# The end of the last token group: order of the sums, columns in two banks, stores of 64 rows

## The chip, the cores and the metric

The kernel runs on one core of a Trainium2 chip. A core has five engines with a queue each: TensorE (PE, matrix products; its weight loads are listed as PEld), VectorE (DVE), ScalarE (ACT), GpSimd (POOL) and SyncE (SP, which only issues transfers here). Transfers are carried by 16 DMA engines that all queues share. The metric is the device time of one execution in microseconds (us), as the median of several runs.

## What is computed

The reference is one block of a network over 2048 tokens of 512 channels: a normalisation with a modulation, a long convolution per channel (computed through a spectrum), a gated residual, and a second normalisation followed by a mixer. What matters for this change is the end of it, the channel MLP of the mixer, in float32:

```python
h2 = _gelu(_layernorm(x1, axis=-1) @ w3) @ w4      # w3: 512 x 1376, w4: 1376 x 512
return x1 + h2
...
x = x + gb * _B_ref(h, B_w1, B_w2, B_w3, B_w4)     # gb: one factor per channel
```

## The kernel before, in words

The tokens lie in one SBUF tile, `X2` (in the profile `KX`), as 128 partitions x 16 blocks x 512 channels. Partition `bp * 32 + q` of block `b` holds token `q * 64 + bp * 16 + b`. In DRAM the output has one row of 512 floats (2 KB) per token, so that the 32 partitions of one `bp` in one block are 32 rows that lie 64 rows (128 KB) apart, and the next `bp` begins 16 rows further on.

The last stage, from about 430 us on, is a loop over eight groups of 256 tokens (`chan(g, hl)`, lines 966 to 1067); a group is two blocks, its two token halves `i = 0, 1` of 128 tokens. The order of the work is written out by hand, and each engine takes its instructions in program order. A group does:

- `chan_first` (922 to 934), called as `first(f2)` for f2 = 0 to 5: the product with w3 for 256 of the 1376 hidden channels (96 in the last, f2 = 5) and all 256 tokens. Each product is made of three (`three`, 822 to 828), since every operand is held as a rounded part (`h`) and a rest (`l`): h x h, l x h and h x l, with 256 columns each. Then ScalarE evaluates GELU twice (into `gh`, rounded, and `gf`) and VectorE subtracts (`gl`, line 933).
- `chan_second` (951 to 955), called as `second(f2)`: the product with w4. For each token half `i` one PSUM bank, `acc[i]` (`pa` in the profile), collects the sums of all 11 hidden tiles; a product has 128 tokens as its stationary side and 512 output channels as its columns. `second_high` (936 to 942) adds the two products with `gh`, `second_low` (944 to 949) the one with `gl`. In `chan_second` the order is high of half 0, high of half 1, low of half 0, low of half 1.
- `chan_out` (957 to 964) for each half: VectorE multiplies the sums by the factors `mods[5]` into a scratch tile (line 960) and adds them to the block of `X2` (line 961); then four stores of 32 rows go to the output (line 963), one for each `bp`. In groups 0 to 6 all are issued on SP, in group 7 alternately on SP and ACT.

Between these, a group prepares the next one: `chan_split`, `chan_mod`, `chan_w2`, `chan_stats`, `chan_norm`, `chan_add`, and in groups 1 to 3 a piece of the token mixing, whose results go to a scratch tensor in DRAM (`GD`, line 837) and come back as windows (`chan_load`, line 860). Those transfers are on SP, in the same queue as the stores. `chan_sum` (874) sums the product with w2 in a bank named `ph`.

In group 7 the end is written out (lines 1059 to 1064): after `first(5)` come the high products of part 4 for both halves, then for half 0 low of part 4, high and low of part 5, then the same for half 1; part 4 has two hidden tiles, part 5 one. Only then both halves' `chan_out` follow.

How a store's address pattern is written: `dram(t, offset, [[step, count], ...])` gives steps and counts from the outermost to the innermost, so `[[64 * 512, 32], [1, 512]]` are 32 rows of 512 floats. Loads and stores elsewhere have 128, 96, 64, 32 or 16 as their outermost count, and the four loads into `DS` (line 331), one row each, have 1.

Of the kernel before, what the change touches and what calls it, by code (L numbers as in the profile page):

```python
# [7 lines left out]
F32 = mybir.dt.float32  # L8
# [99 lines left out]
def dram(t, off, ap):  # L108
    return bass.AP(tensor=t.tensor, offset=t.offset + off, ap=ap)


def body(ctx, tc, A):
    nc = tc.nc
    V, S, P, T, Y = nc.vector, nc.scalar, nc.gpsimd, nc.tensor, nc.sync
# [63 lines left out]
    X2 = KX.rearrange("p (b d) -> p b d", b=16)  # L178
# [9 lines left out]
    ph = a1.enter_context(pool("ph"))  # L188
# [14 lines left out]
    mods = [modu[:, k] for k in range(3)] + [modg[:, k] for k in range(3)]  # L203
# [73 lines left out]
    f2 = lambda t: t.rearrange("p a b -> p (a b)")  # L277
# [190 lines left out]
    def products(k):  # L468
        t, u = divmod(k, 4)
        tr = trig.pop(k)  # L470
        mg = PE[t][0][u]
        e0 = wk.tile([128, 2, 2, 512], F32, name="e0")
        e1 = wk.tile([128, 2, 16, 32], F32, name="e1")
        for a in range(2):
            V.scalar_tensor_tensor(e0[:, 1, a], tr[:, 1, 0], 1.0 - 2.0 * a, mg[:, a], op0=OP.mult, op1=OP.mult)  # L475
        if k == 0:
            weigh(0)
        if u % 2 == 0:
            m1 = m1s[0] = wk1.tile([128, 2, 512], F32, name="m1")
            pt = PE[t][1][:, u:u + 2].rearrange("p a d c -> p (a d) c")  # L480
            V.tensor_mul(m1.rearrange("p a (d x y) -> p (a d) x y", x=4, y=8),
                         pt[:, :, None, :8].to_broadcast([128, 32, 4, 8]),
                         pt[:, :, 8:12, None].to_broadcast([128, 32, 4, 8]))
        V.tensor_mul(e0[:, 0], tr[:, 0, 0:1].to_broadcast([128, 2, 512]), mg)  # L484
        V.tensor_mul(e1.rearrange("p r d q -> p r (d q)"), tr[:, :, 1], m1s[0][:, u % 2:u % 2 + 1].to_broadcast([128, 2, 512]))  # L485
        return e0, e1
# [29 lines left out]
    for k in range(8):  # L516
        w, i = ("w3", k) if k < 4 else ("w4", k - 4)
# [21 lines left out]
    with tc.manual_schedule():  # L539
# [13 lines left out]
        for k in range(33):  # L553
# [8 lines left out]
            if k < 32:  # L562
# [3 lines left out]
                e = products(k)  # L566
# [236 lines left out]
    def mix_mod1(g):  # L803
        mh[g] = (cm.tile([128, 2, 512], F32, name="h2"), cm.tile([128, 2, 2], F32, name="mv"),
                 cm.tile([128, 2], F32, name="rs"), cm.tile([128, 2], F32, name="nm"))
        for i in range(2):
            mod1(mh[g][0][:, i], 2 * g + i)

    def mix_mod2(g, i):
        h, mv, r, nm = mh[g]  # L810
        mod2(h[:, i], 2 * g + i)
        stats(mv[:, i], h[:, i])
        rstd(r[:, i:i + 1], mv[:, i, 1:2])
        P.tensor_tensor(nm[:, i:i + 1], mv[:, i, 0:1], m_one[:, :1], op=OP.mult)
        P.tensor_tensor(nm[:, i:i + 1], nm[:, i:i + 1], r[:, i:i + 1], op=OP.mult)

    def mix_norm(g):
        h, mv, r, nm = mh[g]
        for i in range(2):
            act(h[:, i], h[:, i], AF.Identity, scale=r[:, i:i + 1], bias=nm[:, i:i + 1])  # L820
# [101 lines left out]
    def chan_first(hl, f2):  # L922
        p = psw.tile([128, 2, 256], F32, name="pm")
        ne, m = (2, 128) if f2 < 5 else (1, 96)
        for e in range(ne):
            c = slice((f2 * 2 + e) * 128, (f2 * 2 + e) * 128 + m)
            three(p[:m, e], W3h, W3l, hl, c)
        gf = c2p.tile([128, 2, 256], F32, name="gf")
        gh = c2p.tile([128, 2, 256], F32R, name="gh")
        gl = c2p.tile([128, 2, 256], F32R, name="gl")  # L930
        act(gh[:m, :ne], p[:m, :ne], AF.Gelu_apprx_tanh)
        act(gf[:m, :ne], p[:m, :ne], AF.Gelu_apprx_tanh)
        V.tensor_sub(gl[:m, :ne], gf[:m, :ne], gh[:m, :ne].bitcast(F32))  # L933
        return gh, gl, ne, m

    def second_high(acc, part, f2, i):
        gh, gl, ne, m = part
        s = slice(i * 128, i * 128 + 128)
        for e in range(ne):
            f = f2 * 2 + e  # L940
            T.matmul(acc[i], gh[:m, e, s], W4h[:m, f], start=(f == 0), stop=False)  # L941
            T.matmul(acc[i], gh[:m, e, s], W4l[:m, f], start=False, stop=False)  # L942

    def second_low(acc, part, f2, i):
        gh, gl, ne, m = part
        s = slice(i * 128, i * 128 + 128)
        for e in range(ne):
            f = f2 * 2 + e
            T.matmul(acc[i], gl[:m, e, s], W4h[:m, f], start=False, stop=(f == 10))  # L949

    def chan_second(acc, part, f2):
        for i in range(2):
            second_high(acc, part, f2, i)
        for i in range(2):
            second_low(acc, part, f2, i)

    def chan_out(g, acc, i, qs):
        b = 2 * g + i
        o = c2p.tile([128, 512], F32, name="gf")
        V.tensor_mul(o, acc[i], mods[5])  # L960
        V.tensor_add(X2[:, b], X2[:, b], o)
        for bp in range(4):
            qs[bp % len(qs)].dma_start(dram(A["out"], (bp * 16 + b) * 512, [[64 * 512, 32], [1, 512]]),
                                       X2[bp * 32:(bp + 1) * 32, b])

    def chan(g, hl):
        t = g + 3 if 0 < g < 4 else None
        nx = g + 1 if g < 7 else None
        acc = [psm.tile([128, 512], F32, name=f"pa{i}", bufs=1) for i in range(2)]
        part, st = {}, {}  # L970

        def first(f2):
            part[f2] = chan_first(hl, f2)

        def second(f2):
            chan_second(acc, part.pop(f2), f2)

        def mod(i):
            if t is not None:
                if i == 0:  # L980
                    mix_mod1(t)
                    mix_mod2(t, 0)
                else:
                    mix_mod2(t, 1)
                    mix_norm(t)

        def turn():
            if t is not None:
                st["hl"] = parts_of(transposed(mh.pop(t)[0]))

        def half(hf):
            if t is not None:
                mix_half(t, st["hl"], hf)
                if t < 6:
                    first_stat(2 * t + 2 + hf)

        def nxt(f, *a):
            if nx is not None:
                return f(nx, *a)

        if g == 0:
            first(0)
            split_w(4)
            first(1)
            split_w(2)
            second(0)
            chan_split(1)
            first(2)
            split_w(2)
            chan_mod(1, 0)  # L1010
            second(1)
            chan_mod(1, 1)
            first(3)
            split_w(4)
            second(2)
            chan_w2(1)
            chan_stats(1)
            first(4)
            n = chan_norm(1)
            split_w(3)  # L1020
            second(3)
            chan_add(1)
            first(5)
            r = parts_of(transposed(n))
            second(4)
            chan_load(2)
            second(5)
        else:
            first(0)
            mod(0)  # L1030
            first(1)
            mod(1)
            second(0)
            nxt(chan_split)
            first(2)
            nxt(chan_mod, 0)
            second(1)
            turn()
            nxt(chan_mod, 1)
            first(3)  # L1040
            half(0)
            second(2)
            nxt(chan_w2)
            nxt(chan_stats)
            first(4)
            n = nxt(chan_norm)
            nxt(chan_add)
            half(1)
            second(3)
            first(5)  # L1050
            r = parts_of(transposed(n)) if nx is not None else None
            if g < 7:
                second(4)
            if g < 6:
                chan_load(g + 2)
            if g < 7:
                second(5)
            else:
                second_high(acc, part[4], 4, 0)
                second_high(acc, part[4], 4, 1)  # L1060
                for i in range(2):
                    second_low(acc, part[4], 4, i)
                    second_high(acc, part[5], 5, i)
                    second_low(acc, part[5], 5, i)
        for i in range(2):
            chan_out(g, acc, i, (Y,) if g < 7 else (Y, S))
        return r

    splits = []
# [8 lines left out]
    def split_w(n):  # L1078
        for _ in range(n):
            splits.pop(0)()  # L1080

    steps = [(jh, kc) for jh in range(2) for kc in range(8)]
    with tc.manual_schedule():
# [115 lines left out]
        W4h, W4l, ldw4 = weights(pw34, WD["w4"], 1376, 512, "w4", 11)  # L1199
        c2p = ctx.enter_context(tp("c2p", 2))  # L1200
        psm = ctx.enter_context(tp("psm", 2, space=PSUM))
# [69 lines left out]
```

## Time and profile before

| | |
|---|---|
| median of 3 runs | 711.11 us (710.77 to 711.17) |
| the profiled execution's own time | 710.0 us |
| its span in the profile | 708.2 us |
| mean granted TensorE clock | 0.996 |
| DMA traffic | 85.51 MB, mean 121 GB/s |
| the 64 stores of the output | 64 KB each, 60 on SP and 4 on ACT |

The span is the time from the first to the last instruction of the profiled execution; the execution's own time has 1.8 us around it. In rows of the timeline the columns are start, duration, engine, line, operation, output and inputs, shapes, count, and in brackets the engine's idle time before it with what ended it; equal neighbours are merged, so that a row with x3 covers three. "SPq" and "ACTq" are issues of transfers by these engines' queues. In rows of windows the columns are the window, its length, busy time and number of instructions of PE, PEld, DVE, ACT and POOL, the granted clock, the busy share of the 16 DMA engines and their GB/s. In strips (DMA, GB/s) a window is cut into 40 equal slices; a digit is the busy share in tenths. Packets are what the DMA engines move one by one: a row of an output store is a packet, and beside these there are small ones of under 512 bytes that carry no output.

### The profile page before, as it was taken

Reading aid. Unit: us, or ns where it says so; the run is one execution under the profiler, and the core shown is the slowest. Engines: PE = TensorE matmul, PEld = TensorE weight load, DVE = VectorE, ACT = ScalarE, POOL = GpSimd, SP = SyncE. Lnnn points to the kernel's source line nnn. Section 1 sums busy time; section 2 is a strip of 40 time slices with the busy share of each in tenths; the row PEclk is TensorE's granted clock in tenths of the full one; section 3 lists DMA queues with packets and bytes.
Section 4 is the critical chain, followed back from the end, with each engine's and each line's share of the span. In section 5 each row is a group of like instructions: output and inputs, shape, how many; then the busy total and the mean of one; then the engine's idle time right before and its main releaser. Section 6 shows DMA issues by size and latency. Waiting matters only on the chain.

```text
span 708.2 us, 16836 instructions
## 1 busy us (share of the span) xinstructions
PE 670.5 (95%) x7083; PEld 518.3 (73%) x7083; DVE 500.1 (71%) x827; ACT 336.0 (47%) x553; POOL 91.5 (13%) x203
## 2 busy tenths in 40 slices
PE   1899999999999999997999899999999999999997
PEld 0456655666568655654788789899898988989896
DVE  7799999999986765776988868467454536354522
ACT  3878898889956454542444633314132221212120
POOL 4011112021000000000563101001020000000000
PEclk9999999999999999999999999999999999999999
DMA  8903274745349997965559211011110201111011
GB/s 285 285 2 83 65 219 117 199 103 174 84 105 348 252 274 259 300 208 184 189 187 321 65 31 31 16 45 31 39 52 16 60 16 36 25 31 31 0 31 31
DMA packets 56627, 85.51 MB, mean 121 GB/s; under 512 B 5508, under 2 KB 43400, under 8 KB 54888
## 3 DMA queue, kind: packets, MB, share of 16 engines
q1 hardware_dynamic: 52536, 66.87, 33.4%
q0 software_dynamic: 3136, 16.52, 6.7%
q8 instruction: 56, 0.92, 0.6%
q10 hardware_dynamic: 880, 1.05, 0.5%
q14 instruction: 19, 0.16, 0.1%
HBM read 58.20 MB, written 31.85 MB: 127 GB/s over the span
## 4 chain that ended last, share of the span: by engine, by line
PE 46%; DMA 4%; DVE 2%; ACT 1%; SPq 1%; issue 1%; ACTq 0%; DVEq 0%
PE pm L825 7%; PE pm L826 7%; PE pm L828 7%; PE pa L949 6%; PE pa L941 6%; PE pa L942 6%; PE ph L880 2%; PE ph L882 2%; PE ph L879 2%; DMA GD<-go 2%; PE pT L790 2%; DMA ld<-ZT 1%; DMA w4l<-Dw 1%; PE pT L1139 1%; SPq L738 1%
## 5 line engine op out<-in xcount | busy, mean ns | idle before, releaser
L120 ACT ACTIVATE gh<-pm 128x512 fp32r<-128x512 f32 (+1 forms) x48 | 26.9, 561 | 200.6 <-PE pm L828 200.6
L825 PE MATMUL pm<-nh,w3h 128*128 128x256 f32 (+1 forms) x352 | 85.8, 279 | 0.9 <-ACT nh L120 0.9
L826 PE MATMUL pm<-nh,w3l 128*128 128x256 f32 (+1 forms) x352 | 85.7, 279 | 0.1
L933 DVE TENSOR_TENSOR gl<-gf,gh 128x512 fp32r<-128x512 f32 (+1 forms) x48 | 30.8, 642 | 68.4 <-ACT gf L120 68.4
L941 PE MATMUL pa<-w4h,gh 128*128 128x512 f32 (+1 forms) x176 | 69.6, 396 | 0.0
L942 PE MATMUL pa<-w4l,gh 128*128 128x512 f32 (+1 forms) x176 | 68.9, 392 | 0.0
L825 PEld LDWEIGHTS pm<-nh,w3h 128*128 128x128 f32 (+1 forms) x352 | 65.3, 185 | 2.6 <-ACT nh L120 1.1
L826 PEld LDWEIGHTS pm<-nh,w3l 128*128 128x128 f32 (+1 forms) x352 | 65.3, 185 | 2.2 <-DVE w3l L744 0.5
L828 PE MATMUL pm<-nl,w3h 128*128 128x256 f32 (+1 forms) x352 | 54.8, 277 | 0.0
L949 PE MATMUL pa<-w4h,gl 128*128 128x512 f32 (+1 forms) x176 | 48.1, 390 | 0.8 <-DVE gl L933 0.8
L457 PE MATMUL xx<-MG,ON 64*128 64x512 f32 x160 | 48.1, 397 | 0.0
L458 PE MATMUL xx<-MG,ON 64*128 64x512 f32 x160 | 48.0, 396 | 0.0
L753 POOL TENSOR_TENSOR rs<-mv,eps_t 128x1 f32<-128x1 f32 (+1 forms) x39 | 11.9, 306 | 277.8 <-DVE mv L759 265.8
L828 PEld LDWEIGHTS pm<-nl,w3h 128*128 128x128 f32 (+1 forms) x352 | 46.7, 185 | 0.2 <-DVE nl L798 0.2
L885 DVE TENSOR_TENSOR h<-h,ph 128x512 f32<-128x512 f32 x16 | 11.0, 687 | 45.1 <-PE ph L882 45.1
L475 DVE SCALAR_TENSOR_TENSOR e<-tr,p 128x512 f32<-128x512 f32 x64 | 41.0, 682 | 1.5 <-ACT tr L120 1.4
L120 ACT ACTIVATE z<-pz 128x512 f32<-128x512 f32 x32 | 17.4, 595 | 51.9 <-issue 25.1
L678 DVE TENSOR_TENSOR ma<-pk,us 128x512 f32<-128x512 f32 x32 | 21.9, 685 | 27.3 <-issue 16.1
L507 PEld LDWEIGHTS kp<-e,e 128*32 128x32 f32 x2048 | 30.1, 110 | 12.7 <-issue 8.2
L949 PEld LDWEIGHTS pa<-w4h,gl 128*128 128x128 f32 (+1 forms) x176 | 33.0, 188 | 8.3 <-DVE gl L933 1.2
L484 DVE TENSOR_TENSOR e<-tr,p 128x1024 f32<-128x1024 f32 x32 | 38.9, 1216 | 0.0
L485 DVE TENSOR_TENSOR e<-tr,m 128x1024 f32<-128x1024 f32 x32 | 38.9, 1216 | 0.0
(230 smaller groups left out, 1758.3 us busy)
## 6 DMA issues: line engine op xcount, KB each, us to landing
VU<-vs SPq DMA_DIRECT2D x64, 128.0 KB, 3.4
ld<-VU SPq DMA_DIRECT2D x16, 512.0 KB, 14.5
ZT<-z POOLq DMA_DIRECT2D x15, 512.0 KB, 6.3
ld<-ZT SPq DMA_DIRECT2D x12, 512.0 KB, 6.2
Dw<-in_w POOLq DMA_DIRECT2D x8, 688.0 KB, 4.7
xu<-in_u SPq DMA_DIRECT2D x16, 256.0 KB, 8.1
KX<-in_u SPq DMA_DIRECT2D x16, 256.0 KB, 12.6
GD<-go SPq DMA_DIRECT2D x16, 256.0 KB, 2.2
```

Of the source, the lines that this page charges most:

```text
L120: return S.activation(out, in_, f, bias=bias, scale=scale)
L457: T.matmul(x[:, :512], la, ma, start=(i == 0), stop=(i == len(ops) - 1))
L458: T.matmul(x[:, 512:], lb, mb, start=(i == 0), stop=(i == len(ops) - 1))
L475: V.scalar_tensor_tensor(e0[:, 1, a], tr[:, 1, 0], 1.0 - 2.0 * a, mg[:, a], op0=OP.mult, op1=OP.mult)
L484: V.tensor_mul(e0[:, 0], tr[:, 0, 0:1].to_broadcast([128, 2, 512]), mg)
L485: V.tensor_mul(e1.rearrange("p r d q -> p r (d q)"), tr[:, :, 1], m1s[0][:, u % 2:u % 2 + 1].to_broadcast([128, 2, 512]))
L825: T.matmul(p, wh[:, k, c], hi[k], start=(k == 0), stop=False)
L826: T.matmul(p, wl[:, k, c], hi[k], start=False, stop=False)
L828: T.matmul(p, wh[:, k, c], lo[k], start=False, stop=(k == 3))
L941: T.matmul(acc[i], gh[:m, e, s], W4h[:m, f], start=(f == 0), stop=False)
L942: T.matmul(acc[i], gh[:m, e, s], W4l[:m, f], start=False, stop=False)
L949: T.matmul(acc[i], gl[:m, e, s], W4h[:m, f], start=False, stop=(f == 10))
```

## The change

In group 7 the sums of the second half are kept in two banks: columns 0 to 255 in the old `acc[1]`, columns 256 to 511 in a tile of the `ph` buffers (`acc[3]`). Products of the second half therefore have 256 columns, and there are twice as many. The parts of the last group are (half 0, 512 columns), (half 1, columns 0 to 255), (half 1, columns 256 to 511).

After `first(5)` each part in turn gets all that is left of its sums (high and low of part 4, high and low of part 5), and its `chan_out` follows at once: multiply, add and stores of that part alone.

In all groups `chan_out` stores 64 partitions at a time instead of 32: the address pattern in DRAM gets a dimension in front, `[2, 32, columns]`, for two neighbouring `bp`. In groups 0 to 6 a half has two stores on SP instead of four; in group 7 each part has one on SP and one on ACT.

```diff
-    def second_high(acc, part, f2, i):
+    def second_high(acc, part, f2, i, c=slice(0, 512)):
         gh, gl, ne, m = part
-        s = slice(i * 128, i * 128 + 128)
+        s = slice(i % 2 * 128, i % 2 * 128 + 128)
         for e in range(ne):
             f = f2 * 2 + e
-            T.matmul(acc[i], gh[:m, e, s], W4h[:m, f], start=(f == 0), stop=False)
-            T.matmul(acc[i], gh[:m, e, s], W4l[:m, f], start=False, stop=False)
+            T.matmul(acc[i][:, c], gh[:m, e, s], W4h[:m, f, c], start=(f == 0), stop=False)
+            T.matmul(acc[i][:, c], gh[:m, e, s], W4l[:m, f, c], start=False, stop=False)
...
+    halves = [(0, slice(0, 512)), (1, slice(0, 256)), (3, slice(256, 512))]
 
     def chan_second(acc, part, f2):
-        for i in range(2):
-            second_high(acc, part, f2, i)
-        for i in range(2):
-            second_low(acc, part, f2, i)
-
-    def chan_out(g, acc, i, qs):
-        b = 2 * g + i
+        todo = halves if len(acc) > 2 else [(0, slice(0, 512)), (1, slice(0, 512))]
+        for i, c in todo:
+            second_high(acc, part, f2, i, c)
+        for i, c in todo:
+            second_low(acc, part, f2, i, c)
+
+    def chan_out(g, acc, i, c=slice(0, 512)):
+        b = 2 * g + i % 2
         o = c2p.tile([128, 512], F32, name="gf")
-        V.tensor_mul(o, acc[i], mods[5])
-        V.tensor_add(X2[:, b], X2[:, b], o)
-        for bp in range(4):
-            qs[bp % len(qs)].dma_start(dram(A["out"], (bp * 16 + b) * 512, [[64 * 512, 32], [1, 512]]),
-                                       X2[bp * 32:(bp + 1) * 32, b])
+        V.tensor_mul(o[:, c], acc[i][:, c], mods[5][:, c])
+        V.tensor_add(X2[:, b, c], X2[:, b, c], o[:, c])
+        for h in range(2):
+            (Y, Y if g < 7 else S)[h].dma_start(
+                dram(A["out"], (h * 32 + b) * 512 + c.start, [[16 * 512, 2], [64 * 512, 32], [1, c.stop - c.start]]),
+                X2[h * 64:h * 64 + 64, b, c])
 
     def chan(g, hl):
...
         acc = [psm.tile([128, 512], F32, name=f"pa{i}", bufs=1) for i in range(2)]
+        if g == 7:
+            acc += [None, psm.tile([128, 512], F32, name="ph")]
...
-                second_high(acc, part[4], 4, 0)
-                second_high(acc, part[4], 4, 1)
-                for i in range(2):
-                    second_low(acc, part[4], 4, i)
-                    second_high(acc, part[5], 5, i)
-                    second_low(acc, part[5], 5, i)
-        for i in range(2):
-            chan_out(g, acc, i, (Y,) if g < 7 else (Y, S))
+                for i, c in halves:
+                    second_high(acc, part[4], 4, i, c)
+                    second_low(acc, part[4], 4, i, c)
+                    second_high(acc, part[5], 5, i, c)
+                    second_low(acc, part[5], 5, i, c)
+                    chan_out(g, acc, i, c)
+        for i in range(2 if g < 7 else 0):
+            chan_out(g, acc, i)
         return r
```

`second_low` is changed like `second_high`.

More of the change, by code (lines that the diff above doesn't have):

```diff
@@ L934, in chan_first @@
         return gh, gl, ne, m
-    def second_high(acc, part, f2, i):
+    def second_high(acc, part, f2, i, c=slice(0, 512)):
         gh, gl, ne, m = part
-        s = slice(i * 128, i * 128 + 128)
+        s = slice(i % 2 * 128, i % 2 * 128 + 128)
         for e in range(ne):
             f = f2 * 2 + e
-            T.matmul(acc[i], gh[:m, e, s], W4h[:m, f], start=(f == 0), stop=False)
-            T.matmul(acc[i], gh[:m, e, s], W4l[:m, f], start=False, stop=False)
-    def second_low(acc, part, f2, i):
+            T.matmul(acc[i][:, c], gh[:m, e, s], W4h[:m, f, c], start=(f == 0), stop=False)
+            T.matmul(acc[i][:, c], gh[:m, e, s], W4l[:m, f, c], start=False, stop=False)
@@ L945, in second_low @@
+    def second_low(acc, part, f2, i, c=slice(0, 512)):
         gh, gl, ne, m = part
-        s = slice(i * 128, i * 128 + 128)
+        s = slice(i % 2 * 128, i % 2 * 128 + 128)
         for e in range(ne):
             f = f2 * 2 + e
-            T.matmul(acc[i], gl[:m, e, s], W4h[:m, f], start=False, stop=(f == 10))
+            T.matmul(acc[i][:, c], gl[:m, e, s], W4h[:m, f, c], start=False, stop=(f == 10))
+    halves = [(0, slice(0, 512)), (1, slice(0, 256)), (3, slice(256, 512))]
     def chan_second(acc, part, f2):
-        for i in range(2):
-            second_high(acc, part, f2, i)
```

## The prediction

> **What bounds the kernel now.** I read the profile's page first, then the busy time by windows of the last stage, then the timeline of the tail, then the DMA views.
>
> ```profile
> span 708.2 us, 16836 instructions
> PE 670.5 (95%) x7083; PEld 518.3 (73%) x7083; DVE 500.1 (71%) x827; ACT 336.0 (47%) x553; POOL 91.5 (13%) x203
> ```
>
> TensorE is busy for 95% of the span. In windows of 15 us from 415 to 700 (first and last of 19 rows; the first number after the window's length is PE's) it never stops:
>
> ```profile
> 415.00:430.00 15.00, 15.00 (x89) 13.13 (x88) 9.20 (x19) 4.29 (x10) 0.90 (x2) 1.00 0.13 36
> ...
> 685.00:700.00 15.00, 15.00 (x97) 13.57 (x96) 2.38 (x4) 2.83 (x6) 0.00 (x0) 1.00 0.01 1
> ```
>
> So in groups 0 to 6 the stores, adds and loads lie beside TensorE, and only what changes TensorE's own time counts there. After 700 it is a chain: the end of the sums, VectorE, the stores, their landing. The timeline of the tail:
>
> ```profile
> 699.58 0.42 DVE L933 TENSOR_TENSOR gl<-gf,gh 96x256 fp32r<-96x256 f32 x1 [3.03 <-ACT gf L120]
> ...
> 700.53 0.61 PE L949 MATMUL pa<-w4h,gl 128*128 128x512 f32 x2
> ...
> 701.88 0.69 DVE L960 TENSOR_TENSOR gf<-pa,modg 128x512 f32<-128x512 f32 x1 [1.87 <-PE pa L949]
> ...
> 702.60 0.69 DVE L961 TENSOR_TENSOR KX<-KX,gf 128x512 f32<-128x512 f32 x1
> 702.60 0.39 PE L949 MATMUL pa<-w4h,gl 96*128 96x512 f32 x1
> 703.21 0.68 DVE L960 TENSOR_TENSOR gf<-pa,modg 128x512 f32<-128x512 f32 x1
> 703.32 2.16 SPq L963 DMA_DIRECT2D out<-KX  x4
> 703.33 2.17 ACTq L963 DMA_DIRECT2D out<-KX  x4
> 703.93 0.69 DVE L961 TENSOR_TENSOR KX<-KX,gf 128x512 f32<-128x512 f32 x1
> ```
>
> TensorE ends at 702.99 (702.60 + 0.39), VectorE only at 704.62: from 701.88 on VectorE is the chain. The last issue is ACT's at 705.1; its row below says 2.0 us to landing, so 707.1, and the span ends 1.1 later. Then the DMA strips from 703 to 708.2 (40 slices of 0.13 us) and the row with the highest rate:
>
> ```profile
> L963 ACTq DMA_DIRECT2D out<-KX x2: 374/403/432, 704.6 to 705.1; - x2
> ...
> DMA to landing us min/median/max: 2.0/2.0/2.0
> DMA  0000000047999699913798949995100000000000
> ...
> DMA packets 384, 0.52 MB, mean 101 GB/s; under 512 B 128, under 2 KB 128, under 8 KB 384
> 706.00:706.50 0.50, 0.00 (x0) 0.00 (x0) 0.00 (x0) 0.00 (x0) 0.00 (x0) 0.50 0.96 238
> ```
>
> The data starts in slice 8, near 704.07, 0.75 after the issue at 703.32, and is all but through with slice 27, at 706.6: 1.6 us lie between the end of the data and the end of the span. Eight stores left 384 packets: 256 of 2 KB (8 x 32 rows) and 128 small ones, 16 for each store.
>
> **The change part by part.** *Sums in two banks.* In group 7 the 33 products of the second half (11 tiles x 3) become 66 of 256 columns. Prices:
>
> ```profile
> 691.79 0.28 PE L825 MATMUL pm<-nh,w3h 128*128 128x256 f32 x1
> ...
> 694.54 0.39 PE L941 MATMUL pa<-w4h,gh 128*128 128x512 f32 x1
> ...
> 697.28 0.28 PE L825 MATMUL pm<-nh,w3h 128*96 128x256 f32 x1
> ...
> 698.70 0.39 PE L941 MATMUL pa<-w4h,gh 128*128 128x512 f32 x1
> ```
>
> From 691.79 to 694.54 ran 24 products of 256 columns (0.1146 us each), from there to 697.28 twelve of 512 (0.2283). So 66 x 0.1146 - 33 x 0.2283 = +0.03 us. The 96-wide stage up to 698.70, 12 in 1.42 us, is the upper end (+0.27); a gain is excluded, since the same columns stream. I take 0.03, the same form.
>
> *First half first.* Its last product now stands behind 9 products instead of 13, four fewer: 0.91 us earlier. It needs gl of the last part, ready at 700.00 and used at 700.53; that cover of 0.53 us is enough. The first multiply starts at 701.88 - 0.91 + 0.03 = 701.00, the first add at 701.72, its end is 702.41, the store's issue 702.44 instead of 703.32.
>
> *Each part by itself.* VectorE's queue is then mul, add of 512 and twice mul, add of 256; a 256-wide one takes:
>
> ```profile
> L265 DVE TENSOR_TENSOR p<-p,WN 128x256 f32<-128x256 f32 x8 | 3.3, 418 | 0.4 <-ACT WN L120 0.4
> ```
>
> With the steps of the tail (0.72, 0.61, 0.72 at 512, each 0.27 less at 256): 702.33, 702.78 (end 703.20), 703.12, 703.57 (end 703.99). TensorE is through with the first quarter by 702.0 and with the second by 703.02, so VectorE stays the chain by 0.1 us. Issues at 702.44, 703.22 and 704.01 on SP and on ACT, the last 1.1 before today's. Behind each waiting store stand only the later stores and the final waits. Second add and first quarter's store touch other columns of one block; bounds 0 and a wait, taken as 0 (third rival).
>
> *Stores of 64 rows.* Here lies the sum. The new address pattern in DRAM is 2 x 32 rows: its outermost count is 2. Today's is 32. What says how many of the 16 engines carry a transfer? The list of all DMA issues:
>
> ```profile
> DMA packets 56627, 85.51 MB, mean 121 GB/s; under 512 B 5508, under 2 KB 43400, under 8 KB 54888
> ...
> VU<-vs SPq DMA_DIRECT2D x64, 128.0 KB, 3.4
> ...
> DS<-in_dk SPq DMA_DIRECT2D x4, 0.5 KB
> ld<-in_ld SPq DMA_DIRECT2D x1, 2.0 KB, 1.7
> cT<-in_c SPq DMA_DIRECT2D x1, 2.0 KB
> ```
>
> Its 44 rows (first and last shown) count 332 issues. 332 x 16 small packets and 2 x 128 rows of 16 bytes (ld, cT) make 5568; the page has 5508. The 60 missing are 4 x 15: the four DS issues, the only ones whose outermost count (1) is no multiple of 16, left one small packet each. So a transfer does not always use 16 engines; it follows a count of the pattern. In every issue here the outermost count explains the number: 16 where 16 divides it, 1 where it is 1. A count of 2 is not in the trace. It lies between 1 engine and 16; I take 2, nearer to the DS rows, and keep 16 as a rival.
>
> The Trainium skill, "DMA: Bandwidth & Descriptors", section "Why a DMA increments its semaphore by 16 and not by 1", says that a copy goes over the largest number up to 16 that divides the slowest dimension of both sides, on the lowest-numbered engines; by that rule it is 2, the same two for SP and ACT. The DS rows agree with it; no row tests a 2. The same page's "Specifications" put an engine at about 27 GiB/s (29 GB/s); an estimate by that page is 9.0 us for the stores and 716.7 in all.
>
> The last group's stores are 512 KB, so each of two engines moves 262144 bytes. Rates of one engine from three rows: today's stores reach 238 GB/s at 0.96 busy, 15.5 per engine (16.9 us). The store of GD, also from SBUF to DRAM in rows of 1 KB (half of the new bytes are such rows), and the loads at the start:
>
> ```profile
> GB/s 0 0 0 0 0 0 0 0 0 0 0 0 237 346 355 337 337 355 301 64 0 0 0 0 0 0 0 0 0 0 0 0 0 0 0 0 0 0 0 0
> DMA packets 3122, 6.27 MB, mean 392 GB/s; under 512 B 177, under 2 KB 1177, under 8 KB 2994
> ```
>
> 346 / 16 = 21.6 per engine (12.1 us) and 392 / 16 = 24.5 (10.7 us). I take 21.6: two engines alone have no fourteen others beside them, and the form of the packets is nearest. Both ends stay in the range. The data starts at 702.44 + 0.75 = 703.19 and never runs dry, since the first half alone (131072 bytes per engine) takes 6.1 us and the last issue is at 704.01. End 715.3, span 1.6 later, 716.9: **+8.7 us**. The profiled run took 710.0 us, 1.1 under the median of 711.11 shown; on the median the sum is 719.8.
>
> *Stores of groups 0 to 6.* They get as slow: four issues, again 512 KB, 10.7 to 16.9 us.
>
> ```profile
> 433.90 3.63 SPq L963 DMA_DIRECT2D out<-KX  x8
> 453.46 14.35 SPq L837 DMA_DIRECT2D GD<-go  x2
> ...
> 674.04 4.43 SPq L963 DMA_DIRECT2D out<-KX  x8
> ```
>
> The next transfer on SP comes 19.6 us after the first store, group 6's stores are 28 us ahead of the tail. Cost nothing; TensorE's gapless windows hide it. If that cover went, the next group's window load would be late, and TensorE with it.
>
> **The rivals.** *Sixteen engines* (the other side, not slower). If the rows in total, 64, decide, the transfer is spread as today: 256 KB at 238 GB/s from 703.19 to 704.29, then 128 KB to 704.84, then 128 KB to 705.4; span 707.0, **709.9**. For it: a count of total rows explains the 5508 too, DS has one row in all. Against it: in all 332 issues the outermost count suffices. It decides from 8 engines on: to end the data by today's 706.6, 524288 bytes from 703.19 need 154 GB/s, which is 7.1 engines at 21.6. *Two engines at today's rate* (15.5): 16.9 us instead of 12.1, span 721.7, **724.6**. For it: this is the rate of the very rows stored, and both engines read neighbouring partitions. Against it: there 16 engines share what limits them. *The store of the first quarter holds the last add* until it lands: the last two stores start behind an emptied queue: landing (about 0.4 after the data), add 0.42, issue to data 0.75, 1.6 us more, **721.4**. Against it: in the tail above, the add at 703.93 writes the same tile KX while stores of the other block run, and did not wait.
>
> **How the numbers follow.** Two engines: 0.86 (0.58 near 719.8, 0.21 near 724.6, 0.07 near 721.4). Sixteen: 0.13. Something else: 0.01. A measurement of this kernel can tell about 0.2% (1.4 us) from no change; 709.9 is 0.17% under the median, so the 0.13 divide into 0.08 within and 0.05 faster. The two-engine case spans 718.4 (24.5 per engine) to 724.6, with 1.6 for the wait above and 1.0 below for engines that run freer alone: 717.4 to 726.2. That holds some 0.83. Forecast **719.8 us**, slower 0.87, within 0.08, faster 0.05.
>
> **What would show it.** Right: the small packets of the last stores fall from 16 to 2 each; the DMA share after 704 stands near 2/16 = 0.12 at some 43 GB/s for 12 us instead of 0.9; the first multiply starts near 701.0 and the last add ends near 704.0; from the last issue to landing it takes over 10 us; TensorE stays gapless to 700. Wrong: 16 small packets per store and 0.9 of the engines busy (then 709.9), or a gap of TensorE ahead of a group's first product, where slow stores hold SP.

## The result, and the profile after

The changed kernel takes 721.01 us (median), the kernel before 710.94 in the same runs: a ratio of 1.0136, 95% interval 1.0113 to 1.0159. It is slower, by 10.07 us, where 8.7 were forecast. One of the changed kernel's six executions, of 974.38 us at a granted clock of 0.652, was a slow one and is left out of the ratio. The profiled execution took 720.79 us, with a span of 719.0.

The page of the changed kernel, the same lines as before the change:

```profile
span 719.0 us, 16876 instructions
PE 669.6 (93%) x7116; PEld 518.9 (72%) x7116; DVE 500.3 (70%) x829; ACT 335.9 (47%) x553; POOL 92.3 (13%) x203
...
DMA packets 55799, 85.51 MB, mean 119 GB/s; under 512 B 4552, under 2 KB 42700, under 8 KB 54060
```

TensorE's busy time is the same to within 1 us (669.6 against 670.5); the span has grown. The same 85.51 MB leave with 956 fewer small packets: 64 stores with 16 each (1024) have become 34 with 2 each (68). Now the timeline of the tail, columns as before:

```profile
700.24 0.42 DVE L933 TENSOR_TENSOR gl<-gf,gh 96x256 fp32r<-96x256 f32 x1 [3.05 <-ACT gf L120]
...
701.62 0.69 DVE L963 TENSOR_TENSOR gf<-pa,modg 128x512 f32<-128x512 f32 x1 [0.96 <-PE pa L949]
...
702.35 0.69 DVE L964 TENSOR_TENSOR KX<-KX,gf 128x512 f32<-128x512 f32 x1
...
702.96 0.42 DVE L963 TENSOR_TENSOR gf<-pa,modg 128x256 f32<-128x256 f32 x1
...
703.07 2.12 SPq L966 DMA_DIRECT2D out<-KX  x3
703.08 2.94 ACTq L966 DMA_DIRECT2D out<-KX  x3
...
703.41 0.42 DVE L964 TENSOR_TENSOR KX<-KX,gf 128x256 f32<-128x256 f32 x1
...
704.23 0.42 DVE L964 TENSOR_TENSOR KX<-KX,gf 128x256 f32<-128x256 f32 x1
```

That is what the change is written for: the first multiply begins 1.38 us behind the last subtraction (701.62 - 700.24), where it was 2.30 (701.88 - 699.58), and the first stores are issued 2.83 behind it, where it was 3.74. VectorE is through at 704.65. Then come 12.7 us of nothing but transfers, up to 717.3, and 1.7 us to the end of the span. The DMA strips from 703 to 719 (slices of 0.4 us):

```profile
DMA  0002010111101111111111111111111111100000
GB/s 0 0 0 31 5 15 31 41 36 36 15 26 41 31 44 31 33 46 46 51 51 51 49 49 51 46 49 49 49 46 51 46 46 51 46 23 0 0 0 0
DMA packets 396, 0.52 MB, mean 33 GB/s; under 512 B 12, under 2 KB 268, under 8 KB 396
```

From 704.2 to 717.3 the busy share is about 1 in tenths, not 9 (in rows of windows 0.12 from 704.2 to 709.2 and 0.14 from 711 to 716): two engines of 16 work. Six stores left 12 small packets, two each, where eight stores had left 128.

**Where to put the ruler.** Executions of one kernel here lie several us apart (the kernel before: 707.8 to 716.9 over its runs), and the traces show that much of it falls ahead of the last stage: group 0's second multiply begins anywhere from 433.5 to 438.4. So the traces are compared by two lengths: *the groups*, from that multiply to the last subtraction of group 7, and *the tail*, from there to the end of the span. The multiply of the kernel before, then of the changed one:

```profile
433.79 0.68 DVE L960 TENSOR_TENSOR gf<-pa,modg 128x512 f32<-128x512 f32 x1
```

```profile
434.17 0.68 DVE L963 TENSOR_TENSOR gf<-pa,modg 128x512 f32<-128x512 f32 x1
```

Before, the groups are 699.58 - 433.79 = 265.79 and the tail 708.2 - 699.58 = 8.6; after, 700.24 - 434.17 = 266.07 and 719.0 - 700.24 = 18.8. The groups lost 0.28 us, the tail 10.1.

### The profile page after: what moved, and what is told of

Its sections match the earlier page's. It is cut to its first block, busy times and chain, and to the rows that moved or that the text cites. A ratio compares the mean times of both kernels' runs of the same rounds, so it can differ in the third digit from the quotient of the medians.

```text
span 719.0 us, 16876 instructions
## 1 busy us (share of the span) xinstructions
PE 669.6 (93%) x7116; PEld 518.9 (72%) x7116; DVE 500.3 (70%) x829; ACT 335.9 (47%) x553; POOL 92.3 (13%) x203
## 2 busy tenths in 40 slices
DMA packets 55799, 85.51 MB, mean 119 GB/s; under 512 B 4552, under 2 KB 42700, under 8 KB 54060
## 4 chain that ended last, share of the span: by engine, by line
PE 47%; DMA 2%; DVE 2%; ACT 1%; SPq 1%; issue 1%; ACTq 0%; DVEq 0%
PE pm L825 7%; PE pm L826 7%; PE pm L828 7%; PE pa L949 5%; PE pa L941 5%; PE pa L942 5%; PE ph L879 2%; PE ph L880 2%; PE ph L882 2%; PE pT L790 2%; DMA ld<-ZT 1%; DMA GD<-go 1%; PE pT L1145 1%; PE py L722 1%; DMA win<-GD 0%
## 5 line engine op out<-in xcount | busy, mean ns | idle before, releaser
L941 PE MATMUL pa<-w4h,gh 128*128 128x512 f32 (+2 forms) x176 | 68.2, 389 | 0.0
L942 PE MATMUL pa<-w4l,gh 128*128 128x512 f32 (+2 forms) x176 | 67.3, 385 | 0.0
L949 PE MATMUL pa<-w4h,gl 128*128 128x512 f32 (+2 forms) x176 | 47.1, 384 | 0.8 <-DVE gl L933 0.8
L457 PE MATMUL xx<-MG,ON 64*128 64x512 f32 x160 | 47.0, 389 | 0.0
L458 PE MATMUL xx<-MG,ON 64*128 64x512 f32 x160 | 47.0, 389 | 0.0
L678 DVE TENSOR_TENSOR ma<-pk,us 128x512 f32<-128x512 f32 x32 | 21.9, 686 | 28.0 <-issue 18.8
L120 ACT ACTIVATE p<-xx 128x1024 f32<-128x1024 f32 (+1 forms) x40 | 37.5, 980 | 2.1 <-PE xx L258 0.4
```

What stands on the lines that cost most here:

```text
L120: return S.activation(out, in_, f, bias=bias, scale=scale)
L457: T.matmul(x[:, :512], la, ma, start=(i == 0), stop=(i == len(ops) - 1))
L458: T.matmul(x[:, 512:], lb, mb, start=(i == 0), stop=(i == len(ops) - 1))
L941: T.matmul(acc[i][:, c], gh[:m, e, s], W4h[:m, f, c], start=(f == 0), stop=False)
L942: T.matmul(acc[i][:, c], gh[:m, e, s], W4l[:m, f, c], start=False, stop=False)
L949: T.matmul(acc[i][:, c], gl[:m, e, s], W4h[:m, f, c], start=False, stop=(f == 10))
```

## The experiments

The theory (A): the outermost count of a store's address pattern sets how many engines carry it, 2 here. Rivals: the size or the row count of a store (B), and the new order and banks (C). The lengths of all runs, in us, each from one profiled execution; the ratios come from 4 to 12 executions of a kernel, and e10 and e11 were executed once:

| run | stores, outermost count | multiply | subtraction | span | groups | tail | time, ratio to before (interval) |
|---|---|---|---|---|---|---|---|
| before | 32 rows, 32 | 433.79 | 699.58 | 708.2 | 265.79 | 8.6 | |
| after | 64 rows, 2 | 434.17 | 700.24 | 719.0 | 266.07 | 18.8 | 1.0136 (1.0113 to 1.0159) |
| e1_rows32 | 32 rows, 32 | 436.71 | 702.79 | 711.0 | 266.08 | 8.2 | 0.9992 (0.9971 to 1.0013) |
| e2_only_stores | 64 rows, 2 | 435.12 | 700.91 | 719.7 | 265.79 | 18.8 | 1.0172 (1.0146 to 1.0199) |
| e3_first_groups | 64 rows, 2, but group 7 as before | 435.77 | 701.56 | 710.4 | 265.79 | 8.8 | 0.9998 (0.9974 to 1.0022) |
| e4_rows64_one_step | 64 rows, 64 | 433.61 | 699.68 | 707.7 | 266.07 | 8.0 | 1.0004 (0.9986 to 1.0022) |
| e5_rows32_two_steps | 32 rows, 2 | 437.06 | 703.35 | 721.2 | 266.29 | 17.9 | 1.0157 (1.0127 to 1.0187) |
| e6_rows128 | 128 rows, 4 | 433.48 | 699.56 | 712.7 | 266.08 | 13.1 | 1.0064 (1.0044 to 1.0083) |
| e8_order_only | 32 rows, 32 | 435.73 | 701.53 | 709.8 | 265.80 | 8.3 | 1.0000 (0.9982 to 1.0018) |
| e9_rows64_eight | 64 rows, 8 | 436.07 | 702.14 | 711.5 | 266.07 | 9.4 | 1.0006 (0.9989 to 1.0024) |
| e10_near_rows | 64 rows side by side, 2 | 434.37 | 700.38 | 719.1 | 266.01 | 18.7 | one execution |
| e11_one_queue | 64 rows, 2, all on SP | 438.44 | 704.24 | 722.9 | 265.80 | 18.7 | one execution |

### Undoing the stores alone: e1_rows32

```diff
-        for h in range(2):
-            (Y, Y if g < 7 else S)[h].dma_start(
-                dram(A["out"], (h * 32 + b) * 512 + c.start, [[16 * 512, 2], [64 * 512, 32], [1, c.stop - c.start]]),
-                X2[h * 64:h * 64 + 64, b, c])
+        for bp in range(4):
+            (Y, Y if g < 7 else S)[bp % 2].dma_start(
+                dram(A["out"], (bp * 16 + b) * 512 + c.start, [[64 * 512, 32], [1, c.stop - c.start]]),
+                X2[bp * 32:bp * 32 + 32, b, c])
```

> The changed kernel with the old stores of 32 rows (outermost count 32), order and banks as changed. Theory A, that the outermost count of 2 puts each store on two DMA engines: every store leaves 16 small packets again, the data after 703 runs at over 200 GB/s and ends near 706; with the last issue some 0.6 us earlier than in the kernel before and 0.3 us lost to products of 256 columns, 710.2 to 710.7 us. Theory C, that the new order and the two banks cost the time: it stays near 721.

Measured: 711.12 us. Its DMA strip (703 to 721, slices of 0.45 us) and packets:

```profile
GB/s 0 0 0 0 0 0 0 82 205 292 180 148 135 125 0 0 0 0 0 0 0 0 0 0 0 0 0 0 0 0 0 0 0 0 0 0 0 0 0 0
DMA packets 576, 0.53 MB, mean 29 GB/s; under 512 B 192, under 2 KB 448, under 8 KB 576
```

Twelve stores, 192 small packets, 16 each; the data is through in 3 us. The loss is gone, so C falls. The median is 0.4 above the range expected, on runs that scatter by more, and the rate, expected over 200 GB/s, is so in two slices and 125 to 180 in the last four. By the lengths the new order gains 0.4 in the tail and loses 0.28 ahead of it.

### The stores alone: e2_only_stores

The kernel before, with this in `chan_out`:

```diff
-        for bp in range(4):
-            qs[bp % len(qs)].dma_start(dram(A["out"], (bp * 16 + b) * 512, [[64 * 512, 32], [1, 512]]),
-                                       X2[bp * 32:(bp + 1) * 32, b])
+        for h in range(2):
+            qs[h % len(qs)].dma_start(dram(A["out"], (h * 32 + b) * 512, [[16 * 512, 2], [64 * 512, 32], [1, 512]]),
+                                      X2[h * 64:h * 64 + 64, b])
```

> The kernel before with the new stores of 64 rows (outermost count 2) and nothing else. Theory A: two small packets per store, the last 512 KB start near 704.1 and take 12 to 13.5 us, 719.5 to 722 us, as slow as the whole change. Theory C: near 711.

Measured: 721.99 us. The strip and the packets from 703 to 721:

```profile
GB/s 0 0 0 0 0 0 23 14 14 32 46 36 32 41 27 36 32 27 36 50 50 50 55 50 50 55 50 50 50 50 50 50 55 50 5 0 0 0 0 0
DMA packets 264, 0.52 MB, mean 29 GB/s; under 512 B 8, under 2 KB 8, under 8 KB 264
```

The stores alone make the whole loss: four of them in the last group, eight small packets, the same tail of 18.8. The first ones are issued 3.74 us behind the subtraction (704.65 - 700.91), 0.9 later than in the changed kernel, and the tail is no longer for it: beside stores this slow, the new order brought nothing.

### Sixty-four rows with an outermost count of 64: e4_rows64_one_step

```diff
-                dram(A["out"], (h * 32 + b) * 512 + c.start, [[16 * 512, 2], [64 * 512, 32], [1, c.stop - c.start]]),
+                dram(A["out"], (h * 1024 + b) * 512 + c.start, [[16 * 512, 64], [1, c.stop - c.start]]),
```

> The changed kernel with stores of 64 rows at one step in DRAM, so that the pattern is 64 x columns with an outermost count of 64; for that the tokens land in another order of rows. Theory A: 16 small packets per store, all engines, 709.4 to 710.4 us. Theory B, that a store of 64 rows and 128 KB is slow by its size or by its row count: near 721.

Measured: 710.27 us. As many stores of as many rows and bytes as in the changed kernel; the same stretch:

```profile
GB/s 0 132 182 360 182 219 91 0 0 0 0 0 0 0 0 0 0 0 0 0 0 0 0 0 0 0 0 0 0 0 0 0 0 0 0 0 0 0 0 0
DMA packets 480, 0.52 MB, mean 29 GB/s; under 512 B 96, under 2 KB 352, under 8 KB 480
```

96 small packets on six stores, 16 each, and the shortest tail of all, 8.0. Size and row count do no harm; B falls.

### Thirty-two rows with an outermost count of 2: e5_rows32_two_steps

The old number of rows and stores, in two steps:

```diff
+        for bp in range(4):
+            (Y, Y if g < 7 else S)[bp % 2].dma_start(
+                dram(A["out"], (bp * 512 + b) * 512 + c.start, [[16 * 512, 2], [32 * 512, 16], [1, c.stop - c.start]]),
+                X2[bp * 32:bp * 32 + 32, b, c])
```

> The changed kernel with stores of 32 rows whose pattern is 2 x 16 x columns with two steps that can't be joined (outermost count 2); the tokens land in another order of rows. Theory A: two small packets per store and two engines, the same 512 KB at the end in 12 to 14 us, 719.5 to 723 us. Theory B: 32 rows are as quick as in the kernel before, 710 to 711.

Measured: 721.7 us, twelve stores and 24 small packets. Two pairs decide: the changed kernel and e4 differ only in how a store of 64 rows is addressed, e1 and e5 only in how a store of 32 rows is, and in both the outermost count of 2 is the slow side. The packets from 703 to 721, and the timeline of its queues:

```profile
DMA packets 408, 0.52 MB, mean 29 GB/s; under 512 B 24, under 2 KB 280, under 8 KB 408
```

```profile
706.18 8.03 SPq L966 DMA_DIRECT2D out<-KX  x6
706.18 9.62 ACTq L966 DMA_DIRECT2D out<-KX  x6
```

The issues wait here, too: six took 8.03 us on SP and 9.62 on ACT, in e1 2.67 and 2.84. SP's last two begin at 709.9 and 713.6, although VectorE was through at 707.8.

### The slow stores where TensorE covers them: e3_first_groups

The kernel before, with the stores of e2 in groups 0 to 6 only:

```diff
+        if g < 7:
+            for h in range(2):
+                Y.dma_start(dram(A["out"], (h * 32 + b) * 512, [[16 * 512, 2], [64 * 512, 32], [1, 512]]),
+                            X2[h * 64:h * 64 + 64, b])
+            return
```

> The kernel before with stores of 64 rows (outermost count 2) in groups 0 to 6 only; group 7 as before. If TensorE hides the slow stores of these groups: 710 to 711.5 us, and the time from the last subtraction of group 7 to the end of the span is 8.6 us as in the kernel before. If slow stores hold back SP's queue and so the next group: a gap of TensorE ahead of a group, and 712 us or more.

Measured: 710.55 us, groups 265.79, tail 8.8 (8.6 expected). Ahead of the last group the slow stores cost nothing that can be seen.

### Four and eight engines: e6_rows128 and e9_rows64_eight

e6 stores each part at once, e9 in two steps:

```diff
+        (Y if g < 7 or c.start == 0 else S).dma_start(
+            dram(A["out"], b * 512 + c.start, [[16 * 512, 4], [64 * 512, 32], [1, c.stop - c.start]]), X2[:, b, c])
...
+                dram(A["out"], (h * 1024 + b) * 512 + c.start, [[16 * 512, 8], [128 * 512, 8], [1, c.stop - c.start]]),
```

> The changed kernel with one store of 128 rows for each part, an address pattern of 4 x 32 rows in DRAM (outermost count 4). Theory A: four small packets per store and four engines; the last 512 KB take 5.4 to 6.5 us instead of 13, 713.5 to 715 us. Theory B, the size of a store: at least as slow as 721.

> The changed kernel with stores of 64 rows whose pattern is 8 x 8 x columns with two steps that can't be joined (outermost count 8); the tokens land in another order of rows. Theory A: eight small packets per store; at 24.5 GB/s per engine the data keeps pace with the parts, 710.3 to 711.5 us, about the break-even that the prediction put at 7 to 8 engines. Theory B: near 721.

Measured: 715.27 us with four, 711.91 with eight (before, beside them: 711.28). The strip and the packets of e6, then of e9 (703 to 721):

```profile
GB/s 0 50 5 14 23 59 64 91 100 91 93 98 98 93 100 91 61 34 0 0 0 0 0 0 0 0 0 0 0 0 0 0 0 0 0 0 0 0 0 0
DMA packets 396, 0.52 MB, mean 29 GB/s; under 512 B 12, under 2 KB 268, under 8 KB 396
```

```profile
GB/s 0 0 0 0 0 0 0 91 86 168 134 180 191 173 141 0 0 0 0 0 0 0 0 0 0 0 0 0 0 0 0 0 0 0 0 0 0 0 0 0
DMA packets 432, 0.52 MB, mean 29 GB/s; under 512 B 48, under 2 KB 304, under 8 KB 432
```

Three stores and 12 small packets are four each; six and 48 are eight each. In windows of their quick stretches the changed kernel moves 49 GB/s (711 to 716) at a busy share of 0.14, e6 97 (707 to 710) at 0.27 and e9 183 (708 to 709.5) at 0.53: about two, four and eight engines of 16, at 24.5, 24 and 23 GB/s each. As e6 and e9 also have two steps that can't be merged, it is the count that matters and not the second step. The tail falls from 18.8 to 13.1, 9.4 and 8.0. Both times came out 0.3 to 0.4 above the range expected; the kernel before, beside them, stood 0.3 above its earlier median, and the slow beginning of the transfers (below) was not priced in.

### The order without the columns: e8_order_only

```diff
-    halves = [(0, slice(0, 512)), (1, slice(0, 256)), (3, slice(256, 512))]
+    halves = [(0, slice(0, 512)), (1, slice(0, 512))]
...
-        if g == 7:
-            acc += [None, psm.tile([128, 512], F32, name="ph")]
```

with the stores of e1.

> The new order in group 7 (first half finished and stored first), with the second half whole in its one bank, products of 512 columns, and stores of 32 rows. If the products of 256 columns cost the 0.3 us that the traces show and the columns bring only part of it back: from the last subtraction to the end of the span some 8.2 us (8.6 before), none lost ahead of it, 710.1 to 710.7 us. If the columns were worth their price: 8.6 us, no change against the kernel before.

Measured: 710.81 us, 0.1 above the range expected, ratio 1.0000. By the lengths (265.80 and 8.3) the order alone is as good in the tail as order and columns, and saves the 0.28. Against the kernel before that is 0.3 us, 0.05%, far below what the times can tell; the two profiles with the old group 7 (before and e3) differ by 0.2 themselves. No version here beats the kernel before measurably.

### Far-apart rows or two queues as causes of the slow beginning: e10_near_rows and e11_one_queue

Both are e2 with one edit more, e10 the first line below and e11 the second:

```diff
+            qs[h % len(qs)].dma_start(dram(A["out"], (b * 128 + h * 64) * 512, [[512, 2], [1024, 32], [1, 512]]),
...
+            chan_out(g, acc, i, (Y,))
```

> The kernel before with stores of 64 rows on two engines (outermost count 2, two steps), but the 64 rows of a store lie side by side in DRAM (128 KB in one piece) instead of 128 KB apart; the tokens land in another order of rows. It asks why the last stores on two engines move some 30 GB/s in their first 5 us and 50 GB/s after. Theory D, the far-apart rows of the first block are slow when first touched: 50 GB/s from the start, the data through in 10.7 us instead of 13, the span 2 us shorter behind the last subtraction (16.8 instead of 18.8). Theory E, the pace at which a store begins on its engines: the same 30 GB/s first, 18.8 us.

> The kernel before with stores of 64 rows on two engines, all of group 7 issued on SP. If two queues on the same two engines hinder each other at the start (theory F): 50 GB/s from the start, 16.8 us behind the last subtraction. Under D and E: slow first, near 18.8 us.

Measured, in one execution each: 720.85 and 724.72 us (the kernel before, beside them: 709.86), with tails of 719.1 - 700.38 = 18.7 and 722.9 - 704.24 = 18.7. What e11 takes longer falls ahead of the last stage (its multiply is at 438.44). The strip of e10 (703 to 721), then that of e11 (703 to 723, slices of 0.5 us):

```profile
GB/s 0 0 0 0 0 27 9 14 41 46 36 32 32 27 50 36 27 36 55 50 50 50 55 50 50 50 55 50 50 50 50 55 32 0 0 0 0 0 0 0
```

```profile
GB/s 0 0 0 0 0 0 0 0 0 0 0 0 25 8 12 45 49 41 37 53 49 45 53 49 49 53 41 37 25 49 53 33 37 49 49 53 45 8 0 0
```

Rows that lie side by side begin just as slowly, so D falls. With one queue the rate is up after 1.5 us, but dips again several times, and the tail is the same: the shorter tail that F forecast isn't there, though the beginning did change. E's forecast of a rate of 30 GB/s at first holds in e10 and not in e11, so it isn't shown either.

The two engines don't stand idle in the slow stretch. From 705.8 to 710.8 e2 moved 77 packets at a busy share of 0.13, from 712 to 717 128 packets at the same 0.13, nearly all of them rows of 2 KB: each row took longer at first. And 69 of the 77 were of SP's queue, so ACT's stores had hardly begun. Why a row takes longer at first stays open.

## Why the prediction was right

The result, +10.1 us, lies inside the range, on the side and by the mechanism that were forecast. By its steps:

- *TensorE bounds all up to 700, the slow stores of groups 0 to 6 are hidden*: right (e3; and in the profile after, TensorE is busy 15.00 of every 15 us from 415 to 700). Group 0's stores there move data from 435.2 to some 448.4, and SP's next transfer is issued at 453.83.
- *First half first*: right. First issue 2.83 us behind the last subtraction; the prediction's 702.44 was 2.86.
- *VectorE in three parts*: right. The last add ends 4.41 behind the subtraction (704.65 - 700.24), the prediction's 703.99 was 4.41. No add waited for a store.
- *Products of 256 columns, +0.03*: mis-sized. Of the six kernels with two banks, five have groups of 266.07 or 266.08; of those without, before, e2, e3, e8 and e11 have 265.79 or 265.80. (e5 with 266.29 and e10 with 266.01 each stand 0.2 above their kind, unexplained.) So 24 of the 33 products, those ahead of the last subtraction, already cost 0.28, and the upper end stated (+0.27 for all) was nearer than the form taken.
- *Outermost count 2, two engines*: right, and the step on which all hung. From the trace the prediction had only 60 missing small packets for it, and the trace could not tell an outermost count from a count of all rows; e4 and e5 told them apart, e6 and e9 give 4 and 8.

What the Trainium skill, "DMA: Bandwidth & Descriptors", section "Why a DMA increments its semaphore by 16 and not by 1", states (the largest number up to 16 that divides, on both sides, the slowest dimension that is not of size 1) agrees with the runs at 2, 4, 8, 32 and 64, by 2, 4, 8, 16 and 16 small packets per store.

- *21.6 GB/s per engine, 12.1 us*: mis-sized by 1 us. From 704.2 to 717.3 the two engines moved 524288 bytes at 20 GB/s each. It is not one rate: about 15 per engine in the first 5 us and 24.5 after. The prediction had both rates, each for the whole transfer; that their mixture came near 21.6 is in part luck. No engine reached the 29 GB/s of the prediction's other estimate (9.0 us): 25.5 was the most (51 GB/s in e2, 712 to 717). The first data came 1.1 us after the issue instead of 0.75 (in e4, on 16 engines, also 1.1). With 0.25 for the columns and 0.1 at the end these make up the 1.7 us between the 8.7 forecast and the 10.4 that groups and tail lost together.
- *The rival with 16 engines, -1.2 us*: its size fell when it was run. e4 gains 0.6 in the tail and pays 0.28 for the columns; e1 gains 0.4. The data of e4 is through some 6.2 us behind the subtraction, where the rival reckoned 5.8 (705.4 - 699.58), and the price of the columns had been put at a tenth.
- *Its break-even at 7 to 8 engines*: somewhat low. With eight the tail is 9.4 against 8.6, and with 16 (e4) 8.0, so by the tail it lies between; the time with eight is not to be told from the kernel before.

## What to carry to other kernels

Before joining two transfers into one, read the outermost count of the joined address pattern. Here counts of 2, 4 and 8, which were left where two steps can't be merged into one, gave just so many DMA engines per store, and counts of 32 and 64 gave 16. Count the small packets per transfer in the profile: in every run here they gave the number of engines, and the busy share of the engines agreed. Joining the stores costs nothing when the joined pattern keeps one step, as in e4, which needs another order of the output's rows; with the rows where they are, the stores of 32 rows (e1) were the quicker form.

The slow stores under a busy TensorE cost nothing here, and the same stores behind the last sum cost 10 us. So look at the last stage first, and measure small effects by lengths inside the trace, not by whole times.

## What was not expected of the hardware

- Two engines do not reach their rate at once: some 30 GB/s in the first 5 us, then 50 (about 25 per engine), at the same busy share. In e11, where all stores come on one queue, dips to 25 to 41 GB/s return between stretches of 45 to 53. The cause is open.
- In the last group of e5, with both queues on two engines, the issues are held up: 8.03 and 9.62 us for six, 2.67 and 2.84 in e1. It is no rule for two engines: eight issues of group 0 took 5.41 us in e5, 3.63 in e1.
- A product of 256 columns costs a little over half of one of 512: ahead of the last subtraction 48 of them take 0.28 us more than the 24 whole ones they replace, 12 ns for each pair, although the 24 products of 256 columns quoted from the profile before had shown 1 ns. Those are products with w3; why the ones with w4 cost more isn't shown.
